# Fifteen block products in another order, five sum chains instead of two banks, and another list of steps

## The chip, the cores and the metric

The kernel runs on one core of one Trainium2 chip. A core has five engines with queues of their own: PE (TensorE, with its weight loads shown apart as PEld), DVE (VectorE), ACT (ScalarE), POOL (GpSimd) and SP (SyncE, which issues most DMAs). They work in parallel and wait for each other by semaphores. The metric is device time in microseconds (us) of one execution; all data is fp32.

## The reference

Two blocks follow each other. The first is a gated linear attention over batch 4, 8 heads, 768 tokens and 48 channels per head: `state = f * state + k (x) v`, `y = q . state`, with `f = sigmoid(f_logit)`. Its output, 4 x 768 x 384, goes through a Fourier mixing block:

```python
X = np.fft.fft(np.fft.fft(x, axis=1), axis=2)
u = x + np.real(X)
un = (u - mean(u)) / sqrt(var(u) + 1e-6)         # over the 384 channels
out = u + np.maximum(un @ w_ch1, 0.0) @ w_ch2    # 384 -> 1536 -> 384
```

## The kernel before, in words

**The order is written out by hand.** `ORDER` (L27) is a string of 720 words. The loop at L951 takes one word after the other and issues a piece of work for it; within an engine, instructions run in the order in which they were issued. So a word's place says which instructions stand ahead of it in every queue that it uses, SP's and POOL's too.

- A number is one step of an attention unit (`attention`, L365, and `outputs`, L542). A unit is two heads of one batch; there are 16, four to a batch. Its steps: gates on ACT (L372), the running sum on DVE (L379), exponentials on ACT (L383), two products on DVE (L391, L392), scores on PE (L400), masking on DVE (L404), values and states on PE with a scan on DVE between them (L559 to L616), a copy out on ACT (L625), a transposition on PE (L636), and on DVE the folding that prepares the transform (L663 to L687). `K` transposes the unit's keys on PE.
- `L` loads inputs (L198). `r` and `R` load a block of the weights in 64-bit form into one of three `raw` buffers (L314), `C` turns it into fp32 (L319): ACT (L281), DVE (L283, L284) and POOL (L285) each take part, and the buffer is free when POOL is done. There are 24 blocks: 12 of w_ch1, then 12 of w_ch2.
- `I` and `Z` set constants on POOL: `I` the array `bound` (L174) that the running sum and the warm-up matmuls read, `Z` the zeros and the indices of the stores. `D` issues eight bf16 matmuls on PE that compute nothing needed (L192). `T` and `S` load and sort the transform's tables.
- `F` is one step of a batch's transform (`fnet`, L703): four words of matmuls `z` (L725) with copies on ACT, then three words with `mix` (L744) and, on DVE, the sum with x and its moments (L800 to L805). `H` is a step of what lies behind it: moments, or one normalised block of 128 tokens, transposed on PE (`turn`, L775, tile `pt`) and copied by ACT into `unT` (L784).
- `P` is one step of the two matrix products of a batch (`projected`, L848), in three calls over pairs of 128-token blocks. Batch 0 uses plain products (L865). Batches 1 to 3 use `hidden` (L825) for un @ w_ch1: 15 words each, nine calls in all. Then seven block products with w_ch2 follow (L888, tiles `fx` and `fz`); their eighth word has only the last sum into x (L922) and a store.
- `B` makes a sum of weight blocks that `hidden` needs, `W` those of w_ch2. `V` and `c` load the weights once more and look for tiny values (L331, L339); `M` (`judge`, L933) puts the findings together: six small DVE instructions, one matmul (L944), two DVE instructions. If it finds any, the kernel computes all once more in a slower form.

**`hidden`** cuts w_ch1 into 3 x 3 blocks of 128x512 and the tokens of a pair into 2 x 3 blocks of 128x128, in a scheme that needs 15 block products instead of the plain 18. A line of `PRODUCTS` (L53) is one product: the sums of token blocks to make first (on DVE, L815, 128x128), the token block and the weight block to multiply (four 128x128 matmuls of N = 128, eight records in the trace), and where the result goes. Products accumulate in PSUM on top of what the bank holds, and after each product the bank is read: by ACT (L841) where it is the first for that part of h, else by DVE, which adds it to h (L843). A part of h that is complete goes through a Relu on ACT (L845). So a bank can't take its next product before the reading of the last one is over. Before, there are two banks, taken in turn for the products 1 to 15: 0, 1, 0, 1 and so on. They are the two tiles of the pool `ps_a` (L121), which attention uses too. The pool `ps_f` (L123) has two tiles as well; z, mix, pt, up, fx and fz share them.

Of the kernel before, what the change touches and what calls it, by code (L numbers as in the profile page):

```python
# [12 lines left out]
C = 128  # L13
# [35 lines left out]

PRODUCTS = (  # L53
    (((6, 1, 4, '+'), (7, 6, 0, '+')), 3, 0, 0, True, 3, '=+', False),
    (((8, 2, 6, '-'),), 4, 5, 1, True, 5, '=+', False),
    (((9, 1, 0, '+'),), 7, 9, 0, True, 0, '=-', False),
    (((10, 1, 2, '-'),), 8, 13, 1, False, 2, '=-', False),
    (((11, 8, 5, '+'), (4, 11, 3, '-'), (1, 4, 0, '-'), (7, 2, 1, '-')), 9, 3, 0, False, 2, '-', False),
    ((), 10, 12, 1, False, 1, '=-', False),
    (((8, 4, 10, '+'),), 7, 2, 0, False, 5, '+', False),  # L60
    ((), 11, 7, 1, False, 4, '=+', False),
    ((), 8, 10, 0, False, 3, '-', True),
    ((), 5, 11, 1, True, 5, '+', True),
    ((), 4, 6, 0, False, 4, '+', True),
    ((), 6, 4, 1, True, 1, '+', False),
    ((), 1, 1, 0, False, 1, '-', True),
    ((), 2, 8, 1, False, 2, '+', True),
    ((), 0, 14, 0, False, 0, '+', True),
)
# [14 lines left out]
def kernel(  # L84
# [740 lines left out]
    def hidden(name, unT, h):  # L825
# [2 lines left out]


        tokens = lambda i: unT[:, i % 3, i // 3 ^ FLIP] if i < 6 else sums[:, i - 6]  # L830
        banks = [ps_a.tile([128, 512], F32, tag="sc", name=f"{name}_{i}") for i in range(2)]
        for made, a, w, bank, new, to, how, complete in PRODUCTS:
            for i, one, two, sign in made:
                add(tokens(i), tokens(one), tokens(two), sign)
            for m in range(4):
                nc.tensor.matmul(banks[bank][:, m * 128:(m + 1) * 128], lhsT=block(w)[:, m * 128:(m + 1) * 128],  # L836
                                 rhs=tokens(a), start=(new and m == 0), stop=True, skip_group_check=True)
            out = h[:, to % 3 * 4:to % 3 * 4 + 4, to // 3 ^ FLIP]
            got = banks[bank].rearrange("p (m n) -> p m n", n=128)
            if how[0] == "=":  # L840
                nc.scalar.activation(out, got, AF.Copy, scale=1.0 if how == "=+" else -1.0)  # L841
            else:
                nc.vector.tensor_tensor(out, out, got, ALU.add if how == "+" else ALU.subtract)  # L843
# [245 lines left out]
```

## Time and profile before

| | |
|---|---|
| median of 3 runs | 533.44 us (530.21 to 533.81) |
| the profiled execution, its own time | 530.86 us |
| its span, first to last instruction | 529.1 us |
| PE busy | 498.8 us (94%) |
| DVE busy | 378.2 us (71%) |
| ACT busy | 224.7 us (42%) |
| POOL busy | 56.5 us (11%) |
| matmuls of `hidden` (L836) | 1080 records, 275 ns the median |
| DVE adds out of PSUM (L843) | 81, 686 ns each |
| ACT copies out of PSUM (L841) | 54, 597 ns each |
| Relu on ACT (L845) | 54, 631 ns each |
| token sums on DVE (L815, 128x128) | 90, about 0.29 us each |

Durations come from one profiled execution, so a sum made of them is held against its 530.86 us. A matmul's record (275 ns) is longer than the distance from one matmul's start to the next, as they are pipelined; the cost of a product is therefore read from starts. In the page's 40 slices each digit is a busy share in tenths, and PEclk is the granted TensorE clock. In a row of the timeline the columns are start and length in us, the engine, the line, the operation, the tiles (written <- read), and the count of merged instructions.

### The profile page before, as it was taken

The numbers are of one execution on the slowest core, as the hardware profiler recorded it, in microseconds if no ns is written. First come the engines' busy times: TensorE is split into PE (matmuls) and PEld (weight loads), VectorE is DVE, ScalarE is ACT, GpSimd is POOL, SyncE is SP. The second block draws the span as 40 slices with busy tenths as digits, with TensorE's granted clock in tenths as the row PEclk, the third lists the DMA queues.
The fourth block names the chain that finished last, engine by engine and source line by source line (L and its number), as shares of the span: only waits on it lengthen the run. The fifth ranks groups of instructions, "written<-read, shape, count | busy, mean of one in ns | idle before, by whom it ended". The sixth has DMA issues, their size and how long they took to land.

```text
span 529.1 us, 13793 instructions
## 1 busy us (share of the span) xinstructions
PE 498.8 (94%) x5854; PEld 456.2 (86%) x5854; DVE 378.2 (71%) x746; ACT 224.7 (42%) x529; POOL 56.5 (11%) x85
## 2 busy tenths in 40 slices
PE   4949889989999999999999999999999999999994
PEld 4838668856899889998999999999999999999994
DVE  4868999969746568588587698678777755666461
ACT  5568567654450351443553444551441404132220
POOL 5231044430001100000001000000000000010000
PEclk9887999999999999999999999999999999999999
DMA  8899176562230010203310042102512311430101
GB/s 236 234 253 292 41 230 199 154 189 76 62 100 23 15 56 2 84 1 90 104 55 31 1 109 70 47 14 78 178 28 62 128 56 46 135 90 0 33 1 36
DMA packets 20505, 48.15 MB, mean 91 GB/s; under 512 B 3409, under 2 KB 6034, under 8 KB 20434
## 3 DMA queue, kind: packets, MB, share of 16 engines
q1 hardware_dynamic: 19186, 43.43, 28.7%
q0 software_dynamic: 1104, 3.54, 1.9%
q8 instruction: 48, 0.79, 0.6%
q14 instruction: 23, 0.19, 0.1%
q10 hardware_dynamic: 144, 0.20, 0.1%
HBM read 42.44 MB, written 4.72 MB: 89 GB/s over the span
## 4 chain that ended last, share of the span: by engine, by line
PE 80%; DVE 4%; DMA 2%; issue 1%; ACT 1%; POOL 0%; DVEq 0%
PE ub L836 24%; PE fx L888 16%; PE fz L888 12%; PE up L865 8%; PE z L725 3%; PE mix L744 3%; PE y L559 2%; PE po L874 2%; DMA raw<-in_w_ch_dram 2%; PE sc L400 2%; PE pt L783 2%; PE y L616 1%; PE ds L599 1%; PE yt L636 1%; PE st L538 1%
## 5 line engine op out<-in xcount | busy, mean ns | idle before, releaser
L843 DVE TENSOR_TENSOR h<-h,ub 128x512 f32<-128x512 f32 x81 | 55.4, 686 | 39.8 <-PE ub L836 39.8
L692 POOL DMA_INDIRECT out_dram<-x,place x16 | 18.0, 1122 | 387.3 <-DVE x L918 279.7
L841 ACT ACTIVATE h<-ub 128x512 f32<-128x512 f32 x54 | 32.2, 597 | 60.4 <-PE ub L836 42.5
L865 PE MATMUL up<-unT,w 128*128 128x256 f32 x216 | 49.5, 381 | 0.6 <-ACT unT L784 0.6
L845 ACT ACTIVATE h<-h 128x512 f32<-128x512 f32 x54 | 34.0, 631 | 34.5 <-DVE h L843 34.5
L836 PE MATMUL ub<-unT,w 128*128 128x128 f32 x360 | 46.9, 280 | 0.0
L888 PE MATMUL fx<-block,h 128*128 128x192 f32 x264 | 46.7, 327 | 0.0
L888 PE MATMUL fx<-w,h 128*128 128x192 f32 x264 | 45.6, 327 | 0.0
L865 PEld LDWEIGHTS up<-unT,w 128*128 128x128 f32 x216 | 40.1, 190 | 6.1 <-ACT unT L784 0.8
L836 PEld LDWEIGHTS ub<-unT,w 128*128 128x128 f32 x360 | 43.3, 191 | 0.8
L888 PEld LDWEIGHTS fx<-block,h 128*128 128x128 f32 x264 | 43.3, 190 | 0.3
L888 PEld LDWEIGHTS fx<-w,h 128*128 128x128 f32 x264 | 42.7, 190 | 0.2
L836 PE MATMUL ub<-wide 128*128 128x128 f32 x288 | 38.3, 280 | 0.1
L836 PE MATMUL ub<-wide,w 128*128 128x128 f32 x288 | 38.2, 280 | 0.1
L285 POOL TENSOR_TENSOR w<-w,raw 128x384 uint32<-128x384 uint32 x24 | 28.5, 1189 | 74.9 <-DVE w L284 38.1
L379 DVE TENSOR_TENSOR_SCAN W<-g,bound 112x768 f32<-112x768 f32 x12 | 21.0, 1752 | 21.3 <-ACT g L373 21.3
L836 PEld LDWEIGHTS ub<-wide,w 128*128 128x128 f32 x288 | 34.6, 191 | 1.1 <-DVE h L843 0.3
L836 PEld LDWEIGHTS ub<-wide 128*128 128x128 f32 x288 | 34.5, 191 | 1.1 <-ACT h L841 0.3
L784 ACT COPY unT<-pt 128x384 f32<-128x384 f32 x24 | 11.3, 488 | 37.3 <-PE pt L783 37.3
L867 ACT ACTIVATE h<-up 128x256 f32<-128x256 f32 x36 | 13.7, 380 | 31.5 <-PE up L865 31.5
L559 PE MATMUL y<-at,v 64*48 64x64 f32 (+1 forms) x768 | 18.9, 229 | 5.6 <-ACT yT L629 5.6
L888 PE MATMUL fz<-w,h 128*128 128x192 f32 x132 | 23.6, 328 | 0.0
(188 smaller groups left out, 989.8 us busy)
## 6 DMA issues: line engine op xcount, KB each, us to landing
raw<-in_w_ch_dram SPq DMA_DIRECT2D x24, 384.0 KB, 4.7
v<-in_v_dram SPq DMA_DIRECT2D x16, 288.0 KB, 5.8
k<-in_w_ch_dram SPq DMA_DIRECT2D x12, 384.0 KB, 3.7
g<-in_w_ch_dram SPq DMA_DIRECT2D x12, 384.0 KB, 3.7
k<-in_qkf_dram SPq DMA_DIRECT2D x14, 288.0 KB, 6.0
g<-in_qkf_dram SPq DMA_DIRECT2D x12, 288.0 KB, 5.3
q<-in_qkf_dram SPq DMA_DIRECT2D x12, 288.0 KB, 4.9
wide<-in_qkf_dram SPq DMA_DIRECT2D x10, 288.0 KB, 5.1
```

The lines of the kernel that those rows point to most:

```text
L285: nc.gpsimd.tensor_tensor(bits, bits, lo, ALU.add)
L379: nc.vector.tensor_tensor_scan(W, g, bound[:R], 0.0, ALU.add, ALU.min)
L559: nc.tensor.matmul(y[FILL[g], c // 3, c % 3 * C + t.start:c % 3 * C + t.stop], lhsT=vals[rows, o:o + (64 if g == 0 else D)], rhs=weights, ...
L692: nc.gpsimd.indirect_dma_start(out=out.rearrange("b s d -> (b s) d"), out_offset=bass.IndirectOffsetOnAxis(ap=place[:, b, i:i + 1], axis=0 ...
L725: nc.tensor.matmul(z[:, cols], lhsT=src[:, j, lo:hi], rhs=tab[:, t, T % 2, cols], start=(i == 0), stop=(i == len(parts) - 1), skip_group_c ...
L744: nc.tensor.matmul(mix[:, o], lhsT=zz[:rows_of[T], T, PLACES[c]], rhs=cd[:rows_of[T], T, :NQ - odd], start=(i == 0), stop=(i == 1))
L836: nc.tensor.matmul(banks[bank][:, m * 128:(m + 1) * 128], lhsT=block(w)[:, m * 128:(m + 1) * 128], rhs=tokens(a), start=(new and m == 0), ...
L841: nc.scalar.activation(out, got, AF.Copy, scale=1.0 if how == "=+" else -1.0)
L843: nc.vector.tensor_tensor(out, out, got, ALU.add if how == "+" else ALU.subtract)
L845: nc.scalar.activation(out, out, AF.Relu)
L865: nc.tensor.matmul(pp[:, :256], lhsT=w1[:, kt, m * 128:(m + 1) * 128], rhs=unT[:, kt], start=(kt == 0), stop=(kt == 2))
L888: nc.tensor.matmul(out, lhsT=h[:, m], rhs=blocks[i][:, m], start=(start and m == 0), stop=(m == H - 1), skip_group_check=True)
```

## The change

`PRODUCTS` is another decomposition of the same 15 products and ten token sums. The column `bank` is a chain now, and there are five: the chains 0 to 4 have 6, 5, 1, 2 and 1 products, in the order 0, 1, 2, 0, 1, 3, 0, 1, 3, 0, 1, 4, 0, 1, 0. Chains 0 and 1 are in the tiles of `ps_a`, as the banks were; 2, 3 and 4 take a tile of `ps_f` when they begin. The first product reads a token sum (block 9) where it read a plain block of unT. The last product is the first and only one for its part of h, so its copy out is the Relu itself. Two weight sums change their sign. And `ORDER` is another list of 720 words, with the same words of each kind.

```diff
--- before.py
+++ after.py
@@ -25,53 +25,53 @@
 
 
 ORDER = (
-    "L0f Z L2f L0k 0 2 I r 0 i 0 L0q D r D D D C 0 L0v D D L1f D C 0 1 0 D L2q D 1 0 L1q L1v K0 0 D 2 L1k "
-    "D D r r D 1 1 C D L2k T 0 D 2 1 L3q L3fk D 1 0 C K1 L4fk L2v 0 2 1 2 1 3 L5fk S 0 2 R 4 1 K2 3 4 L3v "
-    "1 3 3 2 C 5 D 2 2 5 L4qv C 1 4 3 D D 3 2 K3 3 4 1 r 2 L5qv 3 3 D 5 2 3 L6fk 3 5 4 D 4 K5 K4 3 2 4 3 "
-    "C 5 C 4 r F0 4 C r F0 L7fk 6 F0 5 F0 C 4 r F0 4 5 H0 H0 5 C H0 P0 r 6 r L6qv C 5 L7qv P0 6 P0 r C r "
-    "6 P0 C 5 r C 6 P0 r 7 6 F0 P0 7 6 C K6 P0 r B C C r P0 P0 7 r F0 6 P0 7 P0 6 C L8fk C P0 r 7 6 K7 r "
-    "C 7 L9fk P0 H0 r P0 7 r C H0 P0 H0 C 7 L9qv C H0 9 6 7 9 9 P0 P0 L8qv 8 P0 B P0 9 W P0 B 7 9 9 5 B 6 "
-    "P0 B P0 P0 9 K9 P0 8 P0 L11fk P0 8 5 P0 9 B H0 8 P0 P0 9 P0 11 P0 8 9 11 K8 P0 B 8 P0 L11qv 8 7 P0 "
-    "L10fk P0 P0 P0 8 B 11 4 P0 P0 8 P0 P0 11 P0 6 P0 P0 P0 P0 7 B 7 F1 B P0 F1 P0 P0 F1 10 B 10 F1 P0 "
-    "K11 F1 P0 11 8 H1 H1 P0 L10qv 11 F1 P0 10 B P0 10 P0 P0 10 B 10 K10 B P0 P0 B P0 B 10 H1 P0 P1 P1 P1 "
-    "P1 P1 L12fk P1 P1 P1 P1 P1 P1 P1 P1 P1 F1 P1 P1 12 P1 10 9 H1 10 P1 10 8 12 P1 P1 12 L12qv 12 9 11 "
-    "12 11 P1 8 P1 H1 12 11 10 11 P1 H1 H1 P1 P1 P1 P1 P1 P1 P1 L13fk P1 P1 L13qv P1 P1 P1 13 P1 P1 P1 13 "
-    "P1 11 P1 11 12 10 K12 P1 L14fk 12 P1 P1 P1 13 P1 H1 12 P1 P1 P1 P1 14 10 11 P1 F2 P1 F2 P1 P1 13 F2 "
-    "P1 P1 P1 F2 P1 P1 P1 F2 P1 P1 F2 13 12 K13 13 F2 13 P1 L14qv L15fk 13 H2 15 14 13 P1 14 14 H2 P1 P1 "
-    "14 13 14 P1 P1 14 K14 15 P1 15 H2 H2 L15qv 14 H2 P2 14 P2 H2 P2 15 P2 P1 P2 P2 P2 P2 P2 P2 P2 P2 P2 "
-    "P2 P2 12 14 15 H2 V H2 c 13 P2 15 15 K15 12 P2 V 15 V 13 14 P2 V 15 P2 14 15 P2 15 14 P2 15 P2 V c "
-    "P2 P2 P2 P2 P2 15 F3 P2 F3 c P2 c V P2 F3 P2 c P2 P2 V F3 P2 P2 F3 P2 F3 P2 c P2 F3 P2 P2 V c P2 P2 "
-    "P2 P2 P2 H3 c V P2 P2 P2 P2 P2 H3 H3 c P2 V P2 P2 V V c P2 c P2 P2 P2 P2 V P2 c c P2 P2 V P2 P2 P2 V "
-    "P2 P2 P2 P2 V H3 c P3 c V V P3 H3 c P3 P3 P3 P3 P3 P3 P3 P3 P3 P3 P3 c P3 P2 P3 V H3 P3 P3 P3 V P3 "
-    "P3 c P3 P3 P3 P3 V P3 P3 H3 P3 c H3 V P3 c P3 V P3 c c P3 P3 V P3 P3 P3 P3 P3 P3 P3 P3 P3 c P3 c P3 "
-    "P3 P3 P3 P3 P3 P3 M P3 P3 P3 P3 P3 P3 P3 P3 P3 P3 P3 P3 P3 P3 P3 P3 P3 P3 P3 P3"
+    "I L0f D L1f 0 D 0 1 L2f D D D D D L0q L0k D L1k 2 Z 0 D 1 i D D L1q L3q 0 0 0 L0v L3fk D 1 r 1 L2q D "
+    "D L1v L2k 2 0 1 K0 3 0 0 D r 3 r D 2 0 1 1 2 C K1 L2v 1 2 1 C 3 2 C 1 K2 3 L4fk 4 2 r 1 2 L5fk D 4 5 "
+    "L3v 1 3 2 D D T C 2 3 0 L4qv K3 5 3 0 2 3 D 3 2 3 S 2 3 D 3 L6fk 6 R 3 4 F0 5 F0 4 L5qv F0 C F0 5 "
+    "L6qv K4 C r C 4 4 r F0 5 4 H0 H0 r C 4 H0 4 C L7fk r F0 r 7 F0 6 4 P0 C L7qv K5 P0 P0 r C r 5 C P0 r "
+    "7 P0 5 6 4 6 P0 C C P0 5 K6 5 L8fk r C P0 7 7 P0 5 6 r P0 C 8 P0 r 6 r C P0 6 7 C K7 H0 C r 7 P0 r 6 "
+    "C r 6 5 P0 C 6 H0 C P0 B 7 r C 6 r C 7 H0 L9fk L8qv P0 8 P0 P0 9 9 7 9 L9qv 6 P0 P0 P0 P0 9 7 9 K9 "
+    "H0 P0 8 9 P0 P0 7 5 P0 P0 B P0 P0 8 7 B 9 8 4 9 H0 B W P0 P0 P0 9 P0 6 P0 P0 L11fk B P0 11 P0 P0 P0 "
+    "P0 B B P0 11 9 8 K8 7 P0 P0 P0 11 8 F1 F1 F1 P0 P0 B L11qv F1 B P0 8 11 8 F1 11 8 L10fk P0 H1 B 10 B "
+    "K11 P0 P0 P0 P0 L10qv 10 B 10 P0 10 P0 P0 10 H1 11 P0 P0 10 B B P0 B P0 H1 B P0 10 K10 P1 P1 P1 P1 "
+    "P1 P1 P1 P1 L12fk P1 P1 P1 P1 P1 P1 F1 P1 F1 10 8 12 10 P1 8 12 10 12 9 P1 P1 P1 P1 L12qv 12 11 9 12 "
+    "P1 H1 P1 H1 P1 12 11 K12 H1 H1 11 11 H1 L13fk P1 P1 P1 L13qv P1 P1 P1 P1 P1 P1 13 P1 P1 P1 P1 P1 13 "
+    "P1 P1 12 10 P1 P1 13 13 12 10 12 11 P1 P1 P1 11 10 P1 L14fk 14 12 P1 K13 P1 11 F2 F2 P1 P1 14 P1 P1 "
+    "L14qv P1 F2 P1 P1 14 P1 P1 P1 P1 P1 P1 14 F2 13 F2 P1 13 F2 P1 13 F2 P1 13 14 L15fk H2 15 13 14 13 "
+    "K14 P1 15 L15qv 15 P1 P1 P1 14 15 H2 P1 H2 14 H2 P1 P2 14 P2 P2 P2 P2 P2 P2 P2 P2 P2 P2 P2 P2 P2 P2 "
+    "13 14 15 K15 H2 H2 15 15 14 P2 V 15 H2 14 15 13 P2 14 c V 15 12 12 P2 P2 15 P2 15 V P2 P2 15 P2 F3 "
+    "F3 F3 P2 H2 c V P2 P2 P2 V V P2 P2 P2 P2 P2 P2 P2 c P2 c c F3 P2 V F3 V F3 V c P2 P2 F3 P2 P2 P2 P2 "
+    "P2 P2 H3 P2 H3 P2 V P2 P2 H3 P2 c P2 c c P2 P2 V P2 P2 P2 P2 P2 P2 P2 V P2 P2 P2 c c P2 c V V c V P2 "
+    "V P2 P2 V P2 P2 H3 P3 c H3 P3 P3 P3 P3 P3 P3 P3 P3 P3 P3 P3 P3 c P2 P3 P3 H3 c P3 P3 P3 V P3 V P3 V "
+    "c P3 P3 H3 P3 P3 H3 P3 c V P3 P3 P3 P3 P3 P3 P3 P3 V P3 P3 P3 P3 c P3 c P3 P3 P3 P3 P3 P3 P3 P3 P3 "
+    "P3 V P3 c c P3 P3 P3 P3 P3 P3 c V P3 c P3 P3 P3 P3 P3 M P3 P3 P3 P3 P3 P3 P3 P3"
 )
 
 
 
 
 PRODUCTS = (
-    (((6, 1, 4, '+'), (7, 6, 0, '+')), 3, 0, 0, True, 3, '=+', False),
-    (((8, 2, 6, '-'),), 4, 5, 1, True, 5, '=+', False),
-    (((9, 1, 0, '+'),), 7, 9, 0, True, 0, '=-', False),
-    (((10, 1, 2, '-'),), 8, 13, 1, False, 2, '=-', False),
-    (((11, 8, 5, '+'), (4, 11, 3, '-'), (1, 4, 0, '-'), (7, 2, 1, '-')), 9, 3, 0, False, 2, '-', False),
-    ((), 10, 12, 1, False, 1, '=-', False),
-    (((8, 4, 10, '+'),), 7, 2, 0, False, 5, '+', False),
-    ((), 11, 7, 1, False, 4, '=+', False),
-    ((), 8, 10, 0, False, 3, '-', True),
-    ((), 5, 11, 1, True, 5, '+', True),
-    ((), 4, 6, 0, False, 4, '+', True),
-    ((), 6, 4, 1, True, 1, '+', False),
-    ((), 1, 1, 0, False, 1, '-', True),
-    ((), 2, 8, 1, False, 2, '+', True),
-    ((), 0, 14, 0, False, 0, '+', True),
+    (((9, 1, 0, '+'),), 9, 3, 0, 2, '=-', False),
+    (((6, 1, 4, '+'), (7, 6, 0, '+')), 7, 9, 1, 3, '=-', False),
+    (((8, 2, 6, '-'), (11, 8, 5, '+'), (10, 1, 2, '-'), (9, 11, 3, '-'), (1, 9, 0, '-'), (7, 2, 1, '-')), 3, 0, 2, 3, '+', False),
+    (((3, 9, 10, '+'),), 7, 2, 0, 5, '=+', False),
+    ((), 4, 5, 1, 5, '+', False),
+    ((), 10, 12, 3, 1, '=-', False),
+    ((), 3, 10, 0, 3, '-', True),
+    ((), 8, 13, 1, 4, '=+', False),
+    ((), 11, 7, 3, 4, '+', False),
+    ((), 9, 6, 0, 4, '+', True),
+    ((), 6, 4, 1, 1, '-', False),
+    ((), 5, 11, 4, 5, '+', True),
+    ((), 1, 1, 0, 1, '-', True),
+    ((), 2, 8, 1, 2, '-', True),
+    ((), 0, 14, 0, 0, '=+', True),
 )
 
 
 WEIGHTS = (
     (9, 3, 6, 'n'), (10, 2, 6, '-'), (11, 8, 2, '+'), (12, 5, 10, '-'), (12, 12, 4, '-'), (13, 12, 6, '-'),
-    (13, 13, 7, '-'), (14, 9, 0, '+'), (14, 14, 1, '+'), (0, 6, 0, '+'), (4, 7, 4, '+'), (8, 13, 8, '+'),
+    (13, 13, 7, '-'), (14, 9, 0, '+'), (14, 14, 1, '+'), (0, 6, 0, '+'), (4, 7, 4, 'n'), (8, 13, 8, 'n'),
     (3, 3, 10, '-'), (7, 7, 1, '+'), (5, 3, 5, '+'), (6, 6, 1, '-'),
 )
 FLIP = 1
@@ -828,20 +828,27 @@
 
 
         tokens = lambda i: unT[:, i % 3, i // 3 ^ FLIP] if i < 6 else sums[:, i - 6]
-        banks = [ps_a.tile([128, 512], F32, tag="sc", name=f"{name}_{i}") for i in range(2)]
-        for made, a, w, bank, new, to, how, complete in PRODUCTS:
+        opened = set()
+        chains = {i: ps_a.tile([128, 512], F32, tag="sc", name=f"{name}_{i}") for i in range(2)}
+        for made, a, w, chain, to, how, complete in PRODUCTS:
             for i, one, two, sign in made:
                 add(tokens(i), tokens(one), tokens(two), sign)
+            new = chain not in opened
+            opened.add(chain)
+            if chain not in chains:
+                chains[chain] = ps_f.tile([128, 512], F32, tag="f", name=f"{name}_{chain}")
             for m in range(4):
-                nc.tensor.matmul(banks[bank][:, m * 128:(m + 1) * 128], lhsT=block(w)[:, m * 128:(m + 1) * 128],
+                nc.tensor.matmul(chains[chain][:, m * 128:(m + 1) * 128], lhsT=block(w)[:, m * 128:(m + 1) * 128],
                                  rhs=tokens(a), start=(new and m == 0), stop=True, skip_group_check=True)
             out = h[:, to % 3 * 4:to % 3 * 4 + 4, to // 3 ^ FLIP]
-            got = banks[bank].rearrange("p (m n) -> p m n", n=128)
-            if how[0] == "=":
-                nc.scalar.activation(out, got, AF.Copy, scale=1.0 if how == "=+" else -1.0)
+            got = chains[chain].rearrange("p (m n) -> p m n", n=128)
+            first = how[0] == "="
+            if first:
+                kind = AF.Relu if complete else AF.Copy
+                nc.scalar.activation(out, got, kind, scale=1.0 if how == "=+" else -1.0)
             else:
                 nc.vector.tensor_tensor(out, out, got, ALU.add if how == "+" else ALU.subtract)
-            if complete:
+            if complete and not first:
                 nc.scalar.activation(out, out, AF.Relu)
             yield
 
```

## The prediction

> **What bounds the kernel now.** I read the page's first part and the slices, then the windows, then single rows of the timeline.
>
> ```profile
> PE 498.8 (94%) x5854; PEld 456.2 (86%) x5854; DVE 378.2 (71%) x746; ACT 224.7 (42%) x529; POOL 56.5 (11%) x85
> ...
> PE   4949889989999999999999999999999999999994
> ...
> DVE  4868999969746568588587698678777755666461
> ...
> PEclk9887999999999999999999999999999999999999
> ```
>
> ```profile
> 0.00:40.00 40.00, 25.00 (x591) 22.19 (x595) 26.29 (x36) 24.29 (x47) 15.10 (x49) 0.86 0.91 241
> 40.00:120.00 80.00, 72.28 (x1281) 57.79 (x1276) 70.91 (x125) 51.95 (x133) 23.43 (x20) 0.95 0.64 182
> 120.00:212.00 92.00, 91.96 (x948) 79.15 (x950) 65.23 (x118) 34.09 (x92) 6.24 (x4) 1.00 0.16 49
> 212.00:493.00 281.00, 280.28 (x2851) 268.85 (x2843) 199.23 (x430) 107.00 (x245) 10.41 (x11) 1.00 0.22 66
> ```
>
> Behind each window's length stand the busy us of PE, PEld, DVE, ACT and POOL, then clock, DMA share and GB/s. Up to 120 us PE is idle for 15.0 + 7.7 us, while DVE (97 us busy) and the loads set the pace. From 120 us to the end of the products PE is idle for under 1 us: there every start that PE delays is paid in full. But a busy PE may still be stalled, since records overlap. So I look at starts in the last call of `hidden`, and in a call with transform words between its products:
>
> ```profile
> 501.80 1.16 PE L836 MATMUL ub<-wide 128*128 128x128 f32 x8
> ...
> 502.79 1.06 PE L836 MATMUL ub<-unT,wide 128*128 128x128 f32 x8
> ...
> 503.74 1.16 PE L836 MATMUL ub<-unT,w 128*128 128x128 f32 x8
> 503.94 0.69 DVE L843 TENSOR_TENSOR h<-h,ub 128x512 f32<-128x512 f32 x1 [0.26 <-PE ub L836]
> ...
> 504.73 1.11 PE L836 MATMUL ub<-wide,w 128*128 128x128 f32 x8
> ```
>
> ```profile
> 289.90 1.05 PE L836 MATMUL ub<-wide,w 128*128 128x128 f32 x8
> 290.79 1.46 PE L725 MATMUL z<-tab,xs 128*96 128x385 f32 x6
> ```
>
> A product alone takes 0.89 us (289.90 to 290.79); in a run of them the starts are 0.99, 0.95, 0.99 apart. The bank explains it: the product of 502.79 is read from 503.94 (1.15 later) for 0.69, and its bank's next product starts at 504.73, 0.10 behind the reading. So the same bank is taken again after 1.15 + 0.69 + 0.10 = 1.94 us, where two free products need 1.78: **0.16 us lost per pair**. Summing what starts exceed 0.89 by, from product to product, the nine calls lose 0.84, 0.96, 0.27, 1.10, 0.21, 0.88, 0.88, 0.89 and 1.31 us: **7.34 us**. The two small ones have transform words between.
>
> **The chains.** Counts stay: 540 products, 81 DVE adds, 54 ACT copies, 90 token sums. In 0 1 2 0 1 3 0 1 3 0 1 4 0 1 0 a chain comes back after three products, 2.67 us, against 1.94 needed: 0.73 us of slack for an add that stands behind a token sum (0.29) or one other small DVE instruction. Only product 15 follows 13 at distance two: 0.16 in the six calls where no transform word stands between them, 1.0 us. Leaving out nine Relus (0.63 each) frees 5.7 us of ACT, which is 42% busy and late nowhere on this path: nothing. So is the new sign of two weight sums (684 ns against 687).
>
> A rule speaks against this part. The Trainium skill, "TensorE: Matmul & The Clock Gate", section "HAM oscillation — how this bites in real kernels", reports that adding PSUM double buffers to a kernel that had been made dense gave no further gain. By it the chains are worth 0; by the rows above up to 7.3. I follow the rows: there the wait for the bank is visible, start by start.
>
> **The price: the first product needs a sum.** Before, products 1 and 2 read plain blocks, so PE had 1.78 us of work while DVE finished the call before:
>
> ```profile
> 493.49 1.95 PE L836 MATMUL ub<-unT,w 128*128 128x128 f32 x16
> 493.69 0.56 DVE L922 TENSOR_TENSOR x<-fx,x 128x384 f32<-128x384 f32 x1 [1.59 <-PE fx L888]
> 494.17 0.28 DVE L815 TENSOR_TENSOR wide<-unT 128x128 f32<-128x128 f32 x1
> ```
>
> The last sum into x (L922) waits for the last block product; the token sum stands behind it on DVE and ends at 494.45. With 0.10 for the signal, a first product that needs it starts 1.06 us late, and its adds and the rest of the call with it. By the new list: in batch 3's third call nothing covers it, 1.06. In batch 2's third and batch 3's second one group of transpositions (six records, 0.65 us) stands before it on PE: 0.41 each. In the other six K, attention or F words give PE over 1.1 us, or (batch 3's first) L922 was put later: 0. Sum 1.9. Product 4 needs the last of nine sums; it comes 2.4 us after the first product's start, needed at 2.67: 0, but an H or c word among the first three products (0.47 and 0.55 us of DVE) eats that in two calls: 0.4. `M` moves from behind product 3, where a product covered its DVE work, to behind product 15: its six DVE instructions (495.10 to 496.08) now stand between the last add and L944, so PE waits 1.0 + 0.1 and L944 takes 0.31 as before; against 0.2 + 0.31 now, 0.9 more.
>
> Chains in `ps_f`: the tile was last read by L922 or an ACT copy at least one product earlier, and fx comes at least three products after chain 4's: 0. This wait isn't in the trace; if chain 2 waited for a copy each time it would cost up to 0.6 (L841) in nine calls, 5.4; a gain is excluded.
>
> Sum for `hidden`: 7.34 becomes 1.0 + 1.9 + 0.4 + 0.9 = 4.2, **3.1 us less**. Ends: 7.3 less if all stalls go; 4.5 more if all nine calls start 1.06 late (9.5 + 2.3 = 11.8).
>
> **The list up to batch 1.** Here I add up DVE durations of the words in both lists. Work ahead of the first z: 52.7 us before, done at 65.9 (13.2 behind); after, 45.2, as four blocks C come later. SP has 7.0 MB to load up to the gates of unit 4, which at 241 GB/s (first window) arrive at 30 us; with 1.9 of gates and the idle 6.56 us at the start (the first load, in both) I estimate a lag of 10.4 and the first z some 10 us earlier. But the four blocks have to be made up for, and this chain is slow:
>
> ```profile
> 106.77 1.02 POOL w L285
> 107.81 6.04 DMA raw<-in_w_ch_dram
> 113.86 1.16 DVE w L283
> ```
>
> Three buffers: block 24 is loaded when POOL is done with block 21. Block 21's DVE work began at 104.4, block 24's at 113.9, 9.5 later; for 18 to 21 it was 8.3. PE's `po` waits for block 24 (117.07). In the new list DVE has only 5.0 us of other work from 21 to 24, so it waits 3 to 4.5 in its own queue, with the attention steps behind it; I get block 24's DVE work done at 115.5 to 117, against 115.6. PE's work ahead of that `po` is equal (73.3 and 73.2 us), so all later work shifts with it: 0 to 1.4, I take **0.7 more**. Ends: 2.8 less (the lead at the first z kept), 10 more (three rounds of the chain each 3.3 longer).
>
> Warm-up: `Z` now stands behind `I`, so PE's warm-up starts some 2.7 us earlier (4.60 now), and 11 of 21 groups come before the first scores; I estimate 4 us of idle PE after them (2.74 now, to 12.29). The same page, section "What's actually happening", says that after an idle window of about 3.4 us the clock is halved until PE was busy as long. By it the first scores and their neighbours lose 2 us; the row 0 to 40 shows PE busy for 25 of 40 us at clock 0.86, not setting the end. I take 0, and 2 as the upper end.
>
> From there to batch 1 PE is saturated in the old list, and DVE has about 6 us to spare ahead of the first L888 in the new one, though `W` is later: 0, plus or minus 3. `V` and `c` share four buffers on SP's queue; by the new list at least 12 us of PE work lie between a `c` and the `c` four later, against 4.7 us for a load of this kind: no wait on DVE, 0. The stores on POOL keep their places behind L918 and L922: 0. Tail behind the last product: same.
>
> **Sum:** 3.1 less and 0.7 more: 530.86 - 2.4 = 528.5 for the profiled execution. The median of the runs lies 2.6 above it (533.44), so I forecast 533.44 - 2.4 = **531.0 us**.
>
> **Rivals.**
> - *The raw chain decides* (slower): DVE, in order, stands at C words 16 to 24 for loads that can't start. Three rounds, each 3.3 longer than the 8.3 seen, give 10 us, less 3.1: 533.44 + 6.9 = 540.3. It passes +1% when block 24 is done after 124 us. For it: 5.0 us of cover only, SP's queue, which reaches later loads behind each `raw`. Against: 19 blocks have 52 us of DVE work among them. 0.18.
> - *The lead stays* (faster): the earlier transform lets PE fill the gaps before 120 us, 4 us of its 22.7 idle, and the stalls go as computed: 533.44 - 7.1 = 526.3. For it: lag 10.4 against 13.2. Against: the same 24 blocks must be done before `po`. 0.27.
> - *It does not do what it says*: the adds are late for another reason (DVE busy with sums), and starts stay at 0.97: 533.4. Against: DVE idles 0.26 to 1.25 us before each add. 0.1.
> - The forecast: 0.45.
>
> About 1%, 5.3 us, is what a measurement of this kernel tells from no change: under 528.1 or over 538.8. Range 522 to 541: the bounds of `hidden` (-7.3 to +4.5) and the front (-2.8 to +10) don't fall together. Faster 0.3 (the lead, and a little of the forecast), slower 0.18 (the raw chain), same 0.52.
>
> **What would show it.** Right: starts 0.89 apart from product 2 to 13, about 1.05 from 14 to 15; batch 3's third call starting 1.1 us behind its last block product; L944 followed by a gap of about 1 us; block 24's DVE work at 114 to 116. Wrong: starts of 0.95 and more with DVE idle before its adds; chain 2, 3 or 4 waiting at its first matmul; PE idle behind 125 us.

## The result, and the profile after

The changed kernel takes **528.52 us** (median of 20 runs, 526.23 to 531.54); the kernel before, on the same chip, took 531.3 (20 runs, 529.61 to 535.81). The ratio is **0.9933, with a 95% interval of 0.9915 to 0.9951**. A second set of runs gave 0.9966 (0.9948 to 0.9983). By the two ratios it is 0.7 and 0.3% faster, 3.6 and 1.8 us (0.9 to 4.5 with their intervals), which is inside the 1% that the prediction called "same". The forecast was 2.4 us; the 531.0 us that it named were counted from a median of 533.44 for the kernel before, which came out at 531.3. The granted clock does not make the difference: its mean over the second set is 0.979 for this kernel and 0.980 for the one before. The profiled executions stand 3.4 us apart: 530.86 and 527.43 us, spans 529.1 and 525.7.

The page of the changed kernel, its totals and three of its rows of slices:

```profile
PE 494.9 (94%) x5854; PEld 452.8 (86%) x5854; DVE 378.6 (72%) x746; ACT 216.8 (41%) x520; POOL 61.3 (12%) x85
...
PE   6788699989999999999999999999999999999994
...
DVE  4669999868986378588688696679586665565571
...
PEclk9879799999999999999999999999999999999998
```

ACT has nine instructions less (the nine Relus) and 7.9 us less work; PE has the same 5854 matmuls and is busy 3.9 us less. Now the windows, with the same columns as before (length, busy PE, PEld, DVE, ACT, POOL, then clock, DMA share, GB/s):

```profile
0.00:40.00 40.00, 29.58 (x681) 26.30 (x681) 24.56 (x30) 27.13 (x53) 10.90 (x36) 0.88 0.90 230
40.00:120.00 80.00, 70.26 (x1191) 55.30 (x1191) 70.62 (x131) 50.13 (x132) 32.69 (x34) 0.95 0.68 187
120.00:212.00 92.00, 92.00 (x973) 80.45 (x972) 67.57 (x125) 33.95 (x90) 5.75 (x4) 1.00 0.19 57
212.00:490.00 278.00, 275.08 (x2808) 263.50 (x2807) 198.62 (x423) 99.08 (x235) 10.99 (x11) 1.00 0.20 62
```

Up to 120 us PE is busy for 99.8 us instead of 97.3. Behind 212 us it was idle for 0.7 of 281 us; now it is idle for 2.9 of 278. That is new: the list now has places where PE truly waits, and they can be read as waits:

```profile
PE ub L841 <- DVE wide L815: 2.5, 4, 0.9
PE turned L951 <- DVE most L949: 0.7, 1, 0.7
PE z L725 <- DVE x L929: 0.6, 1, 0.6
```

(From 212 us on: who waits for whom, us in total, times, the longest.) The first row is the first product waiting for its token sum, the second is `M`, the third a `z` that waits until L929 has read the bank of fx. No row shows a chain that waits for a tile of `ps_f`. Inside a call the stalls have gone. The end of batch 3's second call, products 13, 14 and then 15, with the add of 13:

```profile
472.51 1.95 PE L841 MATMUL ub<-unT,w 128*128 128x128 f32 x16
...
473.60 0.69 DVE L850 TENSOR_TENSOR h<-h,ub 128x512 f32<-128x512 f32 x1 [0.20 <-PE ub L841]
...
474.35 1.16 PE L841 MATMUL ub<-unT,wide 128*128 128x128 f32 x8
```

Product 15 starts 1.84 us behind product 13: 1.09 + 0.69 + 0.06. Two free products need 1.78, so the one place at distance two costs 0.05 to 0.06.

**Where the time went.** I cut both executions at the first product of `hidden`. Ahead of it: 212.6 us before, 208.6 after, but the new list has one `mix` step (8 matmuls, 1.4 us) later than that point, so 2.6 us are gained there (1.7 of them by chance, as the clock shows below). From there to the last matmul: 309.45 before, 309.92 after, less the same 1.4: 0.9 gained. What follows the last matmul is 7.0 and 7.2. The prediction had it the other way round (0.7 lost ahead, 3.1 gained behind), so its sum was near and its split was wrong.

### The profile page after: what moved, and what is told of

It reads as the page before. It is cut to its first block, busy times and chain, and to the rows that moved or that the text cites. A ratio compares the mean times of both kernels' runs of the same rounds, so it can differ in the third digit from the quotient of the medians.

```text
span 525.7 us, 13813 instructions
## 1 busy us (share of the span) xinstructions
PE 494.9 (94%) x5854; PEld 452.8 (86%) x5854; DVE 378.6 (72%) x746; ACT 216.8 (41%) x520; POOL 61.3 (12%) x85
## 4 chain that ended last, share of the span: by engine, by line
PE 80%; DVE 9%; DMA 4%; issue 2%; ACT 2%; SPq 0%; POOL 0%; DVEq 0%; POOLq 0%; ACTq 0%
PE ub L841 23%; PE fx L895 16%; PE fz L895 12%; PE up L872 6%; PE z L725 4%; PE mix L744 3%; PE y L559 3%; PE po L881 2%; PE sc L400 2%; PE y L616 2%; DMA raw<-in_w_ch_dram 2%; PE pt L783 2%; PE ds L599 1%; PE st L538 1%; DVE W L379 1%
## 5 line engine op out<-in xcount | busy, mean ns | idle before, releaser
L841 PE MATMUL ub<-wide,w 128*128 128x128 f32 x360 | 45.2, 277 | 2.1 <-DVE wide L815 2.1
L841 PEld LDWEIGHTS ub<-wide,w 128*128 128x128 f32 x360 | 42.4, 192 | 3.1 <-PE fx L895 1.2
L852 ACT ACTIVATE h<-h 128x512 f32<-128x512 f32 x45 | 28.3, 630 | 36.9 <-DVE h L850 36.8
L841 PE MATMUL ub<-unT,w 128*128 128x128 f32 x288 | 36.8, 275 | 0.0
L841 PEld LDWEIGHTS ub<-unT,w 128*128 128x128 f32 x288 | 34.5, 192 | 0.1
L841 PE MATMUL ub<-unT,wide 128*128 128x128 f32 x216 | 29.1, 278 | 0.0
L841 PE MATMUL ub<-wide 128*128 128x128 f32 x216 | 28.6, 275 | 0.4 <-DVE wide L815 0.4
L841 PEld LDWEIGHTS ub<-unT,wide 128*128 128x128 f32 x216 | 26.4, 192 | 0.5
L841 PEld LDWEIGHTS ub<-wide 128*128 128x128 f32 x216 | 26.3, 192 | 0.5 <-PE ub L841 0.5
```

The costliest lines, as they stand in the source:

```text
L841: nc.tensor.matmul(chains[chain][:, m * 128:(m + 1) * 128], lhsT=block(w)[:, m * 128:(m + 1) * 128], rhs=tokens(a), start=(new and m == 0) ...
```

## The experiments

The ratio of each is to the kernel before on the same chip (its median lay between 529.6 and 531.3 from one set of runs to the next, so only ratios are compared). Beside it stands the time from the first product of `hidden` to the last matmul in the profiled execution, the **stretch** below. It repeats well: 309.92 and 309.97 for the changed kernel in two executions.

### Chains without the list, list without the chains

`chains_old_list` is the new `PRODUCTS` and `hidden` (and the new signs of the two weight sums) with the old `ORDER`, `banks_new_list` the old ones with the new `ORDER`.

```diff
 # chains_old_list, against after
-ORDER = ("I L0f D L1f 0 D 0 1 L2f D D D D D L0q ...")
+ORDER = ("L0f Z L2f L0k 0 2 I r 0 i 0 L0q D r D D ...")
 # banks_new_list, against before
-ORDER = ("L0f Z L2f L0k 0 2 I r 0 i 0 L0q D r D D ...")
+ORDER = ("I L0f D L1f 0 D 0 1 L2f D D D D D L0q ...")
```

> The new chains alone, with the whole old list. Both theories: 531.3 - 7.0 + 6.8 = 531.1 us; starts 0.89 apart inside the calls, but first products that stand 0.4 to 1.3 us late in seven calls. If the first product's sum costs nothing, 524.3. If the sums' slack of 0.73 us does not suffice, 533 and more.

> The old two banks alone, with the whole new list. Theory A: hidden stalls as before, 0.7 of the front, 0.9 of M moved behind product 15: 531.3 + 1.6 = 532.9 us. Theory B: 531.3 - 4.1 + 0.9 = 528.1 us.

Measured: `chains_old_list` 542.52 us, ratio **1.0249** (1.0219 to 1.0280), stretch 322.61; `banks_new_list` 533.29 us, ratio **1.0055** (1.0033 to 1.0076), stretch 315.53. Each half alone is slower than before, and only together are they faster. On the new list the chains shorten the stretch by 5.6 us (315.53 to 309.92).

On the old list the chains lose 13 us where both theories expected nothing. The waits of PE from 212 us on:

```profile
PE ub L841 <- DVE wide L815: 6.6, 7, 1.0
PE z L725 <- DVE se L681: 2.8, 2, 1.7
PE pt L783 <- DVE un L780: 2.0, 2, 1.3
PE turned L951 <- DVE most L949: 1.8, 1, 1.8
PE ub L841 <- ACT unT L784: 1.5, 2, 0.7
```

By starts, the first products of seven calls come 7.8 us late (6.8 were expected). The next three rows were in no expectation: with the old list the words `F`, `H` and `M` stand among products 2 to 5. DVE has the token sums to make there (six at once for the new product 3, 1.7 us), so PE reaches the matmuls of these words while DVE is still at the sums or at the work queued behind them. Measured against before, some distances from product to product grow, by 11.7 us in sum, nearly all at such words and in the slow clock behind `M`, the ways from one call to the next grow by 6.2, and all other distances shrink by 4.8: 13.1 of the 13.2 us. And `M` costs more than its wait:

```profile
509.66 0.16 DVE L949 SCALAR_TENSOR_TENSOR most<-part,most 112x1 f32<-112x1 f32 x1
509.97 0.38 PE L951 MATMUL turned<-ident,most 128*1 128x128 f32 x2 [1.84 <-DVE most L949]
510.28 1.95 PE L841 MATMUL ub<-wide,w 128*128 128x128 f32 x8
...
512.01 1.92 PE L841 MATMUL ub<-unT,w 128*128 128x128 f32 x8
```

After 1.84 us of idle PE the next product takes 1.73 us to the start of the one behind, instead of 0.89: the granted clock is 0.50 from 510.45 to 513.86.

For `banks_new_list` the waits from 212 us on say what the new list costs without the chains:

```profile
PE turned L944 <- DVE most L942: 1.7, 1, 1.7
PE mix L744 <- DVE x L803: 0.6, 1, 0.6
```

`M` stands behind product 15, which in the old decomposition is read by DVE; in the new one ACT reads it, and the wait is 0.7. The second row, a `mix` that waits for a sum, is gone too with the chains. And two calls (batch 1's third, batch 2's second) whose transform words stood between the products before now wait for their banks 0.4 and 0.5 us more.

### The list cut in two

`front_new` and `rest_new` put the first part of one list ahead of the rest of the other, cut at batch 1's first product, with the new chains; `front_only` is the same cut with the old products. The two heads differ by one F1 there, so it had to be moved. In `front_only` it stands ahead of the last `H1`, in `front_new` five words later, directly ahead of the first product.

```diff
 # front_new; front_only is the same on before, with the F1 five words earlier
-ORDER = new list
+ORDER = new list[:348] + "F1" + old list[349:]
 # rest_new
-ORDER = new list
+ORDER = old list[:349] + new list[348:] without its first F1
```

> The new chains with the new list up to the first word of batch 1's products (348 words, and one F1 that the old list has before that point), then the old list. Theory A (the prediction's split: the gain of 3.1 us is made inside the nine hidden calls and their surroundings, the front list costs 0.7): the old rest makes seven of nine first products wait for the last sum into x and then for the token sum (0.4 to 1.3 us each, 6.8 in all), which eats what the chains save (7.0), so about 531.3 + 0.7 - 0.2 = 531.8 us. Theory B (the lead: PE reaches the first hidden product 4.1 us earlier, and nothing is gained or lost behind it): 531.3 - 4.1 - 0.2 = 527.0 us, first hidden product at 208.6.

> The new chains with the old list up to the first word of batch 1's products, then the new list. Theory A: 531.3 - 3.1 = 528.2 us, first hidden product at 212.6 as before. Theory B: what the chains save in stalls is lost elsewhere behind 212 us, 531.3 + 0.5 = 531.8 us.

> The kernel before with only the new list up to the first word of batch 1's products (and the one F1 that the old list has ahead of that point, put ahead of the last H1); old products, old banks, old list behind. Theory A (prediction): the raw chain makes it 0.7 us slower, ratio 1.001. Theory B (the new front gains what the profiles show at the first hidden product, 4.1 us less the 1.3 us of the F1 step that is missing there, 2.8): ratio 0.995. Theory C (most of these 2.8 us was a half clock in the one profile of before, 1.9 us behind 117 us, which comes by chance): 0.9 us faster, ratio 0.998.

Measured: `front_new` 1.0261 (1.0239 to 1.0283), against 1.0249 with the old head; `rest_new` 1.0028 (1.0007 to 1.0049); `front_only` 1.0039 (1.0019 to 1.0058). Taken at their word these deny any gain of the new head. But the moved F1 is a cost of its own. In `front_only` the last H1 transposition waits for it, and the clock falls towards the end of the wait; the wait, and the 6.8 us from 214.47 on:

```profile
PE pt L783 <- DVE un L780: 2.4, 1, 2.4
```

```profile
214.47:217.88 3.41, 3.02 (x55) 2.60 (x56) 2.71 (x9) 0.96 (x2) 0.00 (x0) 0.50 0.13 35
217.88:221.30 3.42, 3.42 (x18) 3.42 (x17) 0.00 (x0) 1.22 (x2) 0.00 (x0) 0.50 0.60 166
```

2.4 us of wait is more than the 2.1 that were measured. (The profiled execution, 537.79 us, is the slowest of its 22, whose median is 532.43.) In `front_new` the first product waits 2.2 us in the same way. The cut was badly placed, and these three runs settle nothing on the head. There is a better place: in both lists the first 366 words hold each word the same number of times, and both end with the last product of batch 1's first call.

```diff
 # front_366, against before
-ORDER = old list
+ORDER = new list[:366] + old list[366:]
 # rest_366, against after
-ORDER = new list
+ORDER = old list[:366] + new list[366:]
```

> The kernel before with the first 366 words of the new list and the old list behind; the two heads have the same words of each kind and both end with product 15 of batch 1's first call, so nothing has to be stitched. Old products and banks. The cut in front_only cost 2.5 us at one place (a transposition that waits behind an added mix), and 2.0 were measured, so the new head itself should be 0 to 2 us faster than the old: ratio 0.996 to 1.000. The prediction's step (the raw chain makes it 0.7 us slower) gives 1.001 to 1.002.

> The other half of the same cut: the first 366 words of the old list, the new list behind, with the new chains. From the first hidden product to the last matmul the profiles give after 0.8 us less than before for equal work (309.92 less 1.31 for the F1 step that falls in it, against 309.45). If that is all that chains and rest are worth, 0.5 to 1.0 us faster than before, ratio 0.998 to 0.999. If the old head makes the chains of call 1 wait (its first product stands ahead of one transposition more in the run rest_new), no gain, 1.000. If the prediction's 3.1 us are there, 0.994.

Measured: `front_366` 528.51 us, ratio **0.9978** (0.9960 to 0.9996): the new head alone is 1.2 us faster (0.2 to 2.1). `rest_366` 530.53 us, ratio **1.0030** (1.0010 to 1.0049): slower, by 0.5 to 2.6 us. In its trace the stretch is 308.89, 0.6 less than before, but the last H1 transposition now stands directly ahead of call 1's first product, which waits for its sum and comes 1.06 us late. That is an expected loss of 0.5, the lower end of what was measured. The two halves add up to 0.4 us slower; without the 1.06, which the whole change doesn't have, to 0.7 faster. Measured together they are 1.8 to 3.6 faster. With intervals of 1 us on each this is not a contradiction, but by whole executions a part of 1 to 2 us stays unexplained. The traces, read from fixed marks, do add up: 0.9 in the stretch and, as shown below, 1.2 ahead of it, 2.1 us in all.

### Taking away single waits

`sum_early` makes the first product's token sum two words earlier in three calls:

```diff
             product(3, Z, h12)
             tt(c2, X, c2, ALU.add)
+            if not again and (b, j) in ((2, 1), (3, 0), (3, 1)):
+                first_sum(f"ub{b}_{j + 1}", turned_of[b][j + 1])   # the sum of PRODUCTS[0], not made again in hidden
             yield
```

> The kernel after, with the token sum of the first product issued on DVE two words earlier (ahead of the last two sums into x) for three calls: batch 2's third, batch 3's second and third. If the first product's sum is what makes these three start late (0.69, 0.77 and 1.10 us between the last matmul ahead and the first product), 2.5 us less than after: ratio to before 0.9933 - 0.0047 = 0.989. If the starts are late for the transposed blocks or the weights, no change, 0.993.

Measured: ratio 0.9929 (0.9905 to 0.9952), no difference that these runs tell; the stretch is 308.56, 1.4 less and not 2.5. The trace of batch 3's third call shows why:

```profile
491.03 1.05 PE L853 MATMUL ub<-wide,w 128*128 128x128 f32 x8
491.23 0.56 DVE L943 TENSOR_TENSOR x<-fx,x 128x384 f32<-128x384 f32 x1 [1.59 <-PE fx L907]
...
492.02 0.29 DVE L815 TENSOR_TENSOR wide<-wide,unT 128x128 f32<-128x128 f32 x1
...
492.46 1.13 PE L853 MATMUL ub<-wide 128*128 128x128 f32 x8 [0.38 <-DVE wide L815]
```

The first product (491.03) no longer waits for the last sum into x (L943 here). But the two sums of product 2 stand behind it, so product 2 starts 1.43 behind product 1 instead of 0.97. Nearly half of the wait has moved on by one product.

`judge_early` takes `M` apart:

```diff
         nc.vector.scalar_tensor_tensor(most[:R], part[:R, 1:2], WARM, most[:R], ALU.is_ge, ALU.max)
+        yield
         turned = ps_f.tile([128, 512], F32, tag="f", name="turned")
         nc.tensor.matmul(turned[0:1, :128], lhsT=most, rhs=ident, start=True, stop=True)
+        yield
 # ORDER, batch 3's second and third call
-... w1.2 w1.3 w1.4 w1.5 w1.6 w1.7 h2.1 h2.2 V h2.3 c c h2.4 ... c V h2.10 c ... h2.15 M
+... w1.2 c w1.3 c w1.4 c w1.5 c w1.6 M w1.7 h2.1 h2.2 M h2.3 h2.4 M ... h2.15
```

> The kernel after, with the step M cut in three words: its six DVE instructions behind the seventh block product with w_ch2 of batch 3's second call, its matmul behind product 2 of the third call, its last two DVE instructions behind product 4; the last six looks at the weights (c) moved up so that they precede it, into the block products with w_ch2. If M's DVE work between the last add and its matmul costs 0.9 to 1.0 us, as the gap ahead of L951 says: ratio 0.9933 - 0.0018 = 0.9915. If the gap only hides what is late next (the last Relu and the sums of h ahead of the block products), no change.

Measured: ratio 0.9951 (0.9935 to 0.9968), between the two results of the kernel after, so the runs decide nothing. In the trace the wait of L951 is gone and the stretch is 309.11, 0.8 less: the price of `M` was real, and nothing late came up behind it.

`three` does both (with an early sum in batch 2's second call too) and takes the three `z` apart that stood in a row, and `best` issues the sums of product 2 early as well. There `ahead` means the first and second call of batches 2 and 3:

```diff
 # three: batch 2's second call
-... w0.7 F3 F3 F3 h1.1 H2 c V h1.2 h1.3 h1.4 ...
+... w0.7 h1.1 F3 H2 h1.2 F3 c V h1.3 h1.4 F3 ...
 # best, in projected
             product(6, X, h11)
             tt(d2, Z, d2, ALU.add)
+            if ahead: first_sums(f"ub{b}_{j + 1}", turned_of[b][j + 1], 0)   # those of product 1
             ...
             product(3, Z, h12)
             tt(c2, X, c2, ALU.add)
+            if ahead: first_sums(f"ub{b}_{j + 1}", turned_of[b][j + 1], 1)   # those of product 2
```

> The kernel after with both of these (the early sum also in batch 2's second call), and with the three z steps that stood in a row ahead of batch 2's second call put behind its products 1, 2 and 4, so that none waits for the bank of fx or for the copy of the z before. If the three places are independent: 2.5 + 1.0 + 0.6 to 1.2 = 4.1 to 4.7 us less than after, ratio to before 0.985. If z in ps_f between the products holds up chain 2 or 3, the third part turns into a loss of up to 2 us: 0.990.

> The kernel after, unchanged, beside the others on one chip: 0.9933 as before.

> As in the run three, but the sums of products 1 and 2 are both issued early, behind the fifth and sixth block product with w_ch2 of the call before (batch 2's first and second call, batch 3's first and second). In the profile of three the late start had moved on to products 2 and 3, whose sums still stood behind the last sum into x: starts 0.99 and 1.22 apart in batch 3's second call, 1.43 in the third. If DVE then keeps ahead, PE needs 2.3 + 1.1 = 3.4 us less than in after from the first hidden product on: ratio to after 0.9935, to before 0.987. If the early sums push the sums into x and the store, no gain over three.

Measured: `three` 0.9932 (0.9901 to 0.9962), stretch 307.59, 2.3 less than after where 4.1 to 4.7 were expected; 1.0 of what is missing is again the sums of products 2 and 3, and the `z` brought only 0.2 instead of 0.6 to 1.2 (from batch 2's first call to its third 75.66 us, against 75.87 in `sum_early`). `best` **524.8 us** (7 runs, 521.82 to 527.06), ratio to before 0.9908 (0.9868 to 0.9947), beside 528.14 us for the kernel after (`after_again`, 0.9966): 0.6% below it. The stretch is 306.50, **3.4 less than after, as expected**. Batch 3's third call in `best`:

```profile
488.72 1.05 PE L849 MATMUL ub<-wide,w 128*128 128x128 f32 x8
488.92 0.56 DVE L942 TENSOR_TENSOR x<-fx,x 128x384 f32<-128x384 f32 x1 [0.69 <-PE fx L903]
...
489.61 1.06 PE L849 MATMUL ub<-wide 128*128 128x128 f32 x8
...
490.60 0.38 PE L965 MATMUL turned<-ident,most 128*1 128x128 f32 x2
...
490.91 1.16 PE L849 MATMUL ub<-unT,w 128*128 128x128 f32 x8
```

Product 2 starts 0.89 behind product 1, `M`'s matmul 0.99 later takes 0.31 and waits for nothing, and the last sum into x (L942) runs beside product 1. This is the fastest version here.

## Why the prediction was right, and where its steps failed

**The sum was near, its two parts were not.** 2.4 us faster were forecast, 1.8 to 3.6 measured. That the sum came out is luck: the gain in `hidden` was forecast 2.2 us too high (3.1 against 0.9) and the list ahead of it 1.9 us too slow (0.7 slower against 1.2 faster), and the two errors cancel. Point by point:

- *Starts inside a call.* Right: 0.89 from product to product. Only the place at distance two was put too dear: 0.16 per call taken from the old pairs, 0.05 measured, since the add begins 1.09 and not 1.15 behind the product's start. 1.0 forecast, 0.3 found.
- *Chains in `ps_f`.* Right at 0: no wait for such a tile behind 212 us in the profile of after. Neither there nor in before does PE wait for ACT behind 212 us, so the nine Relus less had nothing to shorten, as forecast.
- *The first product needs a sum.* The mechanism is right and its place was named; it was mis-sized. The three calls named lose 1.10, 0.69 and 0.77 (1.06, 0.41 and 0.41 forecast), 2.56 instead of 1.9. The prediction gave the group of transpositions ahead of the first product six records and 0.65 us; an `H` word has three (L783, 24 words and 72 records), 0.33 us, and 1.06 - 0.33 is the 0.7 that was found. This row is batch 3's third call, with the sum behind L929 (for before: 493.69 and 494.17):

```profile
489.20 0.56 DVE L929 TENSOR_TENSOR x<-fx,x 128x384 f32<-128x384 f32 x1 [1.59 <-PE fx L895]
489.67 0.48 DVE L815 TENSOR_TENSOR wide<-unT 128x128 f32<-128x128 f32 x2
490.10 1.13 PE L841 MATMUL ub<-wide,w 128*128 128x128 f32 x8 [0.94 <-DVE wide L815]
```

- *Words among the first three products.* Forecast 0.4 as H and c words. The costly one is an attention step (word 14) behind batch 2's first product: product 2 starts 1.53 behind it. With what is left in small pieces it is 1.8.
- *`M` behind product 15.* The place and the cause are right, the size nearly: a wait of 1.1 was forecast where the old place cost 0.2, and 0.89 was found. (The sum for `hidden` took the difference, 0.9, though its 7.34 holds the old 0.2; in its own terms it should have been 4.4.) The last of its DVE instructions and its matmul, with the block product that follows:

```profile
504.31 0.16 DVE L949 SCALAR_TENSOR_TENSOR most<-part,most 112x1 f32<-112x1 f32 x1
504.61 0.38 PE L951 MATMUL turned<-ident,most 128*1 128x128 f32 x2 [0.72 <-DVE most L949]
504.92 1.89 PE L895 MATMUL fx<-w,h 128*128 128x192 f32 x10
```

- *Sum for `hidden`.* 4.2 forecast, 5.6 found, against 7.3 before: 1.8 gained and not 3.1. The prediction also left out the other words between the calls: three `z` in a row cost 0.8 more than the old spacing. Hence the 0.9 of the cut at the top (1.8 less 0.8), to within 0.1.
- *The list up to batch 1.* **This step failed.** It said 0.7 slower: block 24 of the weights comes later, PE's work ahead of the `po` that waits for it is equal, so all later work shifts; and it put the rest of the way to batch 1 at 0. Block 24 came as said, its DVE work ending at 115.83 (115.5 to 117 forecast, 115.6 before):

```profile
114.87 0.36 DVE L283 TENSOR_SCALAR w<-raw 128x384 uint32<-128x384 uint32 x1 [2.55 <-DMA raw<-in_w_ch_dram]
...
115.96 1.13 POOL L285 TENSOR_TENSOR w<-w,raw 128x384 uint32<-128x384 uint32 x1 [1.71 <-DVE w L284]
...
116.66 4.68 PE L881 MATMUL po<-w,h 128*128 128x384 f32 x14
```

  It acts by another way than the prediction said: on DVE the normalisation `un` (L780) stands behind block 24, and PE waits for `un` with a transposition ahead of `po`. That row, first of before, then of after:

```profile
116.14 0.52 PE L783 MATMUL pt<-ident,un 128*128 128x128 f32 x3 [1.87 <-DVE un L780]
```

```profile
116.28 0.55 PE L783 MATMUL pt<-ident,un 128*128 128x128 f32 x3 [1.88 <-DVE un L780]
```

  So this row comes 0.14 later, not 0.7, and from one execution to the next block 24 moves by more: its DVE work ends between 115.6 and 117.8 in the four profiles with the old head, between 115.3 and 118.0 in the eight with the whole new one. The gain lies behind this transposition. From its start to the first product of `hidden` PE is busy throughout, and the new head takes 92.32 us in seven of its eight profiles (94.01 in `sum_early`, where the clock fell). The old head takes 95.84 to 95.86 in `chains_old_list`, `rest_new` and `rest_366`, of which 0.94 are the wait of the first product for its sum: 94.9 (in before 96.50, of which 1.7 are the slow clock below). Of the difference of 2.6 the `mix` step is 1.4, and **1.2 us** are left, what `front_366` measured. The new list has two groups of transpositions `yt` (0.57 each) fewer behind this point, as it issues them earlier, where PE has idle time (20.2 us up to 120, 22.7 before), and one group `pt` (0.33) more: 0.8 of the 1.2. The other 0.4 stay open. The first `z` came 6.2 us earlier (57.6 against 63.8), not 10.
- *The clock.* The prediction's windows of before held a loss that comes by chance. Two windows, ahead of the fall of the clock in the execution of before and behind it, then two of the same length around the same work in after (cut a whole number of 3.41 us behind its last change of the clock, at 61.26); the number behind POOL's busy time is the granted clock:

```profile
113.92:117.34 3.42, 1.55 (x19) 1.33 (x16) 2.70 (x4) 1.29 (x3) 2.00 (x2) 1.00 0.09 26
117.34:120.75 3.41, 3.41 (x7) 1.76 (x6) 1.80 (x2) 2.10 (x5) 0.00 (x0) 0.50 0.02 5
```

```profile
112.46:115.87 3.41, 1.94 (x72) 1.54 (x69) 0.96 (x3) 1.94 (x5) 1.01 (x1) 1.00 0.82 220
115.87:119.28 3.41, 3.00 (x12) 1.95 (x13) 0.83 (x3) 2.16 (x4) 1.13 (x1) 1.00 0.49 131
```

  Both kernels leave PE idle for 1.87 and 1.88 us ahead of the transposition. In the execution of before the clock then falls to 0.50 for 3.41 us, and `po` matmuls stand 0.64 apart instead of 0.32: 1.7 us. In the profiles of `chains_old_list`, `rest_new` and `rest_366`, with the same head, it did not fall there; in `sum_early`, with the new head, it did. So 1.7 of the 2.6 us between the two profiles ahead of `hidden` are this, and 0.9 remain: the 1.2 less the 0.14 of the row above, to within 0.2.
- *Warm-up.* Forecast 0, at most 2. The clock of the first 40 us is 0.88, against 0.86; no run here tests this step alone.

**The rule on PSUM buffers.** The Trainium skill ("TensorE: Matmul & The Clock Gate", section "HAM oscillation — how this bites in real kernels") saw no further gain from PSUM double buffers in a kernel whose loop had been reordered to keep PE busy. The prediction followed the rows instead, and the runs agree with the rows: on the same list the change of `PRODUCTS` and `hidden`, the price of the first product's sum included, shortens the stretch by 5.6 us, 1.1% of the kernel.

**The rivals.** The raw chain did not decide: block 24 was never done later than 118.6 us in any profile. The lead was partly kept (1.2 us of the 4 that this rival had for the head). That the change doesn't do what it says is refuted by the starts.

## What to carry to other kernels

A hand-written order and the algorithm that it was made for are one thing: of this change each half alone lost 0.5 and 2.5%, and the whole gained 0.3 to 0.7%. When a stall on PE is taken away by moving an instruction on an in-order engine, look at what stands behind the same blocker next: the early sum of one product brought half of its worth, the sums of two brought all. And for effects under 1% compare the traces from a fixed mark (here 309.92 and 309.97 in two executions, and 92.32 us in seven profiles), not whole executions, whose start moved by 3 us.

## What the hardware showed that was not expected

An idle time of 1.84 us ahead of L951 was followed by 3.41 us at a granted clock of 0.50, one of 1.87 us (in before) as well, and one of 2.4 us (in `front_only`) by 6.83 us. Idle times of the same length (1.88 us in after, 1.74 us ahead of a z in `chains_old_list`) were followed by full clock.

The traces show a pattern in this. In all fourteen profiles each change of the clock lies a whole number of 3.41 us behind the change before it. Between 100 us and the end of PE's work the clock fell seven times, and each time PE had been busy for 0.22 to 0.47 of the 3.41 us before. One such stretch of 0.46 (in `front_new`, from 510.23) and all of 0.50 or more were followed by full clock. So what counts here is how much of one such stretch is idle: the 1.87 us of before lie within one (PE busy for 1.55 of 3.42), the 1.88 us of after are divided between two (1.94 and 3.00 of 3.41). This is read from the profiles; no run moved an idle time to test it.

The Trainium skill ("TensorE: Matmul & The Clock Gate", section "What's actually happening") gives a free-running window of about 3.4 us that must be idle. The traces agree with its length and with its running free, but here less than 2 us of idle time were enough. A stretch at half clock cost 1.69 us (94.01 against 92.32 for the same work), so an idle PE of about 2 us can cost nearly twice what the waits show.
